# Smaller PSUM tiles, a new order of convolution bursts, and a moved share of the statistics in a ConvNeXt-V2 block

**Chip, cores, metric.** One core of a Trainium2 chip. The time is device microseconds of one execution, median of several; lower is better.

## The reference

```python
# x: (1, 512, 512, 96) bf16
out = depthwise_conv_3x3(x, dw)
h = layernorm(out, axis=-1)
h = gelu(h @ w1)                                   # 96 -> 384, tanh form
gx = sqrt((h*h).sum(axis=(1, 2)) + 1e-6)           # over all pixels, by channel
nx = gx / (gx.mean(-1) + 1e-6)
h = grn_gamma * (h * nx) + grn_beta + h
return x + h @ w2                                  # 384 -> 96
```

The sum of squares over all pixels is needed before the contraction may start. So the kernel has two phases: phase 1 makes `h` block by block (128 blocks of four rows) for the sum, and phase 2 makes most of `h` again and contracts it.

## The kernel before

`# ...` marks cuts. A block has four quarters of 512 pixels. For channel-major quarters (channels on partitions) VectorE's `bn_stats` gives the sum of squares; for the others (pixel-major) TensorE adds `v.T @ v` to a Gram matrix, whose diagonal is the sum.

```python
def cm_quads(q):                      # channel-major quarters of block q
    return 2 if is_res(q) else 3      # is_res: the last two blocks
# PSUM: psS 1 bank (Gram and layernorm sums, one tile SG),
#       psU 2 tiles of 2 banks, psY 1 tile of 3 banks (convolution)
psU = p1.enter_context(tc.tile_pool(name="psU", bufs=2, space=bass.MemoryType.PSUM))

def burst(n, fence=True):             # 24 matmuls of the convolution
    # ...
    if n < 2 and fence:
        pe.drain()

def pair(j):                          # two quarters of one chunk of 128 channels
    U = psU.tile([128, 2, QW], f32, name="U")
    for t in range(2):
        cm_mm(U[:, t, :], j, t)
    act.activation(out=gsh[:, :, j, :], in_=U[:], func=ACTF.Gelu_apprx_tanh)
# rest(n): the same for 1024 columns of the third and fourth quarter, into gm

def stage_moments(k):                 # once in a batch of four blocks
    # ...
    dve.tensor_scalar(out=m[:, :, :N], in0=S[:, :, :N], scalar1=1.0 / C, scalar2=None, op0=ALU.mult)
    dve.memset(S[:], 0.0)             # S is a part of SG

def combine(b):                       # when 32 entries of bn_stats are full
    # ... for j in range(NCH): dve.bn_aggr(...)

# one slot: convolution of block s beside the expansion of an earlier block b
conv(0); pair(0); conv(1); spread_out(); turn_x(s + 2)
pair(1); squares(0); gram_of_last(0)
pair(2); squares(1); gram_of_last(1)
rest(0); squares(2); stage_turn(k); conv(2); evac()   # evac: y_bf <- Y on ScalarE
rest(1); stage_stats(b2); rest(2); squares_rest()
for b in get("combine"):
    combine(b)                        # then the next slot, first its stage_moments
```

The program gives each engine its instructions in this order.

## Time and profile before

| | before |
|---|---|
| time, median of 3 runs | 1563.49 us (1561.01 to 1563.60) |
| phase 1 and phase 2 | about 1024 us and 535 us |
| one ordinary block of phase 1 | 7.40 us |

### The profile page before, as it was taken

Reading aid. Unit: us, or ns where it says so; the run is one execution under the profiler, and the core shown is the slowest. Engines: PE = TensorE matmul, PEld = TensorE weight load, DVE = VectorE, ACT = ScalarE, POOL = GpSimd, SP = SyncE. Lnnn points to the kernel's source line nnn. Section 1 sums busy time; section 2 is a strip of 40 time slices with the busy share of each in tenths; the row PEclk is TensorE's granted clock in tenths of the full one; section 3 lists DMA queues with packets and bytes.
Section 4 is the critical chain, followed back from the end, with each engine's and each line's share of the span. In section 5 each row is a group of like instructions: output and inputs, shape, how many; then the busy total and the mean of one; then the engine's idle time right before and its main releaser. Section 6 shows DMA issues by size and latency. Waiting matters only on the chain. (4 is left out here: it accounts for less than half of the span.)

```text
span 1559.3 us, 54608 instructions
## 1 busy us (share of the span) xinstructions
PE 1438.9 (92%) x23119; PEld 819.7 (53%) x23119; DVE 1211.7 (78%) x2157; ACT 1436.7 (92%) x1306; POOL 1318.4 (85%) x933
## 2 busy tenths in 40 slices
PE   7889989999999999999999997789999999999998
PEld 3334444444444444444444443357777766676666
DVE  6749989999999999999999999955555555455555
ACT  3779989999999999999999999999999999899997
POOL 3459889989998998898899897459999999899997
PEclk8899999999999999999999999999999999999999
DMA  5568787777778778778868767879999999999996
GB/s 152 162 174 256 241 251 249 223 225 246 228 245 250 231 226 258 237 221 250 244 207 252 221 198 222 275 249 395 380 385 384 381 377 378 341 389 379 376 379 236
DMA packets 235467, 427.86 MB, mean 274 GB/s; under 512 B 34103, under 2 KB 148375, under 8 KB 235223
## 3 DMA queue, kind: packets, MB, share of 16 engines
q1 hardware_dynamic: 219972, 356.59, 70.4%
q0 software_dynamic: 13888, 67.64, 11.5%
q8 instruction: 181, 2.97, 0.8%
q14 instruction: 64, 0.52, 0.1%
q10 hardware_dynamic: 1362, 0.15, 0.1%
HBM read 272.78 MB, written 150.72 MB: 272 GB/s over the span
## 5 line engine op out<-in xcount | busy, mean ns | idle before, releaser
L32 PE MATMUL U<-ynT,w1p 128*128 128x512 bf16 x2292 | 664.4, 381 | 48.5 <-ACT gm L32 10.0
L32 ACT ACTIVATE gr<-U 128x1536 bf16<-128x1536 f32 (+1 forms) x384 | 519.1, 1456 | 13.1 <-PE U L32 11.3
L32 DVE BATCH_NORM_STATS2 bst<-gsh 128x6 f32<-128x512 bf16 x756 | 463.0, 674 | 21.7 <-ACT gsh L32 15.7
L32 DVE TENSOR_TENSOR o_sb<-O,xb 128x384 bf16<-128x384 f32 x512 | 277.9, 556 | 250.7 <-PE O L32 153.0
L32 POOL TENSOR_TENSOR yn<-y_bf,rbc 128x1536 bf16<-128x1536 bf16 x128 | 397.4, 3107 | 87.3 <-ACT rbc L32 31.0
L32 ACT ACTIVATE gsh<-U 128x1024 bf16<-128x1024 f32 x378 | 374.5, 1025 | 61.5 <-PE U L32 61.4
L278 POOL TENSOR_TENSOR xb<-xr,B2c 128x1536 f32<-128x1536 bf16 x126 | 394.8, 3135 | 33.9 <-DVE B2c L32 30.9
L32 ACT ACTIVATE gm<-U 128x1024 bf16<-128x1024 f32 x384 | 381.8, 1047 | 0.2
L32 PE MATMUL Y<-xT,Wq 64*32 64x511 bf16 (+1 forms) x8694 | 324.6, 391 | 32.9 <-ACT y_bf L32 25.8
L32 POOL TENSOR_TENSOR ysq<-y_bf 128x1536 bf16<-128x1536 bf16 x114 | 313.2, 2748 | 32.9 <-ACT y_bf L32 32.4
L32 PEld LDWEIGHTS <-w1p 128*128 128x128 bf16 x2292 | 181.6, 97 | 289.5 <-issue 203.3
L32 PEld LDWEIGHTS <-gr 128*128 128x128 bf16 x4584 | 236.8, 98 | 107.5 <-issue 23.4
L32 PE MATMUL O<-W2s,gr 128*128 128x96 bf16 x4584 | 257.2, 206 | 12.4 <-DVE o_sb L32 11.9
L32 DVE BATCH_NORM_STATS2 bst<-gm 128x6 f32<-128x512 bf16 x378 | 242.3, 679 | 29.7 <-ACT gm L32 29.7
L32 PEld LDWEIGHTS <-Wq 64*32 64x32 bf16 x9216 | 114.0, 91 | 212.5 <-issue 174.1
L32 ACT ACTIVATE y_bf<-Y 128x1536 bf16<-128x1536 f32 x121 | 177.5, 1467 | 16.2 <-PE Y L32 16.1
L32 DVE STREAM_TRANSPOSE xT<-xin 128x576 f32<-128x576 f32 (+1 forms) x256 | 180.4, 745 | 2.1 <-DMA xin<-in_x_dram 2.0
L32 PEld LDWEIGHTS <-gm 128*128 128x128 bf16 x1560 | 106.8, 98 | 66.3 <-issue 11.7
L32 PE MATMUL SG<-gm 128*128 128x128 bf16 x1560 | 126.1, 219 | 8.9 <-DVE SG L32 8.2
L32 PE MATMUL U<-w1p,ynT 128*128 128x384 bf16 (+2 forms) x780 | 126.5, 272 | 5.0 <-ACT gm L32 3.8
L250 POOL DMA_DIRECT2D xr<-in_x_dram x123 | 68.4, 556 | 35.9 <-POOL xb L278 35.9
L32 PEld LDWEIGHTS <-ynT 128*128 128x128 bf16 x780 | 67.3, 97 | 35.3 <-issue 15.4
(103 smaller groups left out, 696.6 us busy)
## 6 DMA issues: line engine op xcount, KB each, us to landing
ynT<-yn_dram SPq DMA_DIRECT2D x254, 384.0 KB
xin<-in_x_dram SPq DMA_DIRECT2D x126, 432.0 KB
yn_dram<-yn SPq DMA_DIRECT2D x512, 96.0 KB
xr<-in_x_dram POOLq DMA_DIRECT2D x128, 384.0 KB, 6.5
out_dram<-o_sb SPq DMA_DIRECT2D x127, 384.0 KB
g_dram<-gsh SPq DMA_DIRECT2D x126, 384.0 KB
gl<-g_dram SPq DMA_DIRECT2D x84, 384.0 KB
gl<-g_dram POOLq DMA_DIRECT2D x42, 384.0 KB, 7.2
```

Source lines behind the costliest of these rows:

```text
L32: r = f(*a, **k)
L250: pq.dma_start(out=xr[:], in_=x[0, r0:r0 + GR].rearrange("r w c -> (r w) c").rearrange("(p g) c -> p g c", g=PXP))
L278: pq.tensor_tensor(out=xb[:], in0=grp[q]["xr"][:], in1=bias[:, None, :].to_broadcast([128, PXP, C]), op=ALU.add)
```

## The change

Its intent: give ScalarE work while TensorE runs a convolution burst. Three tiles (2, 1 and 1 banks) take the place of two tiles of 2 banks. A tile and a half are filled before the second burst instead of one, that burst has no drain behind it, and the Gram matmuls move later. Two channel-major quarters instead of three in every third block take work from VectorE and give it to TensorE; this part is called "the third" below. A "meeting" below is a place where VectorE has the aggregation directly ahead of the moments of a batch.

```diff
     def cm_quads(q):
-        return 2 if is_res(q) else 3
+        return 3 if q % 3 and not is_res(q) else 2
...
-        psU = p1.enter_context(tc.tile_pool(name="psU", bufs=2, space=bass.MemoryType.PSUM))
+        psU2 = p1.enter_context(tc.tile_pool(name="psUa", bufs=1, space=bass.MemoryType.PSUM))
+        psU1 = p1.enter_context(tc.tile_pool(name="psUb", bufs=2, space=bass.MemoryType.PSUM))
+        def banks(n):
+            return (psU2 if n == 2 else psU1).tile([128, n, W], f32, name=f"U{n}")
...                                            (pair and rest become unit(first bank, banks))
                 conv(0)
-                pair(0)
-                conv(1)
+                unit(0, 2)
+                unit(2, 1)
+                squares(0)
+                conv(1, False)
                 spread_out()
                 if s + 2 < NBLK:
                     turn_x(s + 2)
-                pair(1)
-                squares(0)
-                ...                            (gram_of_last(0))
-                pair(2)
+                unit(3, 1)
+                unit(4, 2)
                 squares(1)
-                ...                            (gram_of_last(1))
-                rest(0)
+                gram_of_last(0)
+                unit(6, 1)
                 squares(2)
+                unit(7, 1)
                 ...
                 conv(2)
                 if evac:
                     evac()
-                rest(1)
+                gram_of_last(1)
+                unit(8, 2)
+                unit(10, 1)
                 ...                            (statistics)
-                rest(2)
+                unit(11, 1)
                 squares_rest()
```

More of the change, by code (lines that the diff above doesn't have):

```diff
@@ L260, in fresh, with half @@
                     grp[q]["made"] = late.gr.tile([128, NCH, (NQ - 1) * QW], bf16, name="gr")
-                if is_res(q):
-                    U = psU.tile([128, 2, QW], f32, name="U")
-                else:
-                    U = late.psU2.tile([128, NQ - 1, QW], f32, name="U2")
-                for t in range(nk, NQ):
-                    pe.matmul(quad_out(U[:, t - nk, :]), lhsT=w1p[:, j * 128:(j + 1) * 128],
-                               rhs=quad(ynt[:], t), start=True, stop=True)
-                n = (NQ - nk) * QW
-                act.activation(out=grp[q]["made"][:, j, :n], in_=U[:].rearrange("p k w -> p (k w)")[:, :n],
-                                func=ACTF.Gelu_apprx_tanh)
+                def half(U, t0, t1):
+                    for t in range(t0, t1):
+                        pe.matmul(quad_out(U[:, t - t0, :]), lhsT=w1p[:, j * 128:(j + 1) * 128],
+                                  rhs=quad(ynt[:], t), start=True, stop=True)
+                    act.activation(out=grp[q]["made"][:, j, (t0 - nk) * QW:(t1 - nk) * QW],
+                                   in_=U[:, :t1 - t0, :].rearrange("p k w -> p (k w)"), func=ACTF.Gelu_apprx_tanh)
+                if not is_res(q):
+                    half(late.psU2.tile([128, NQ - 1, QW], f32, name="U2"), nk, NQ)
+                elif j % 2:
+                    half(banks(1), nk, nk + 1)
+                    half(banks(1), nk + 1, NQ)
+                else:
+                    half(banks(2), nk, NQ)
             return [lambda j=j: fresh(j) for j in range(NCH)]
@@ L344 @@
         busy(FILL[0])
-        Ud = psU.tile([128, 2, W], f32, name="U")[:, 0, :NI * 9].rearrange("p (i k) -> p i k", i=NI)
+        Ud = banks(2)[:, 0, :NI * 9].rearrange("p (i k) -> p i k", i=NI)
         for i in range(NI):
@@ L409, in conv_taps @@
             if spare:
-                Ua = psU.tile([128, 2, W], f32, name="U")
-                Ub = psU.tile([128, 2, W], f32, name="U")
+                Ua, Ub = banks(2), banks(1)
                 Y = [Ua[:, 0, :], Ua[:, 1, :], Ub[:, 0, :]]
@@ L538, in stage_spread @@
             wide = rns.pop(k)
-            U = psU.tile([128, 2, W], f32, name="U")
+            U = banks(2)
             for bb in range(n):
@@ L617, in cm_mm, with unit @@
                 pe.matmul(quad_out(dst), lhsT=w1p[:, j * 128:(j + 1) * 128], rhs=quad(yt[:], t), start=True, stop=True)
-            def pair(j):
-                U = psU.tile([128, 2, QW], f32, name="U")
-                for t in range(2):
-                    cm_mm(U[:, t, :], j, t)
-                act.activation(out=gsh[:, :, j, :], in_=U[:], func=ACTF.Gelu_apprx_tanh)
-            def rest(n):
-                U = psU.tile([128, 2, QW], f32, name="U")
+            def unit(bank, n):
+                U = banks(n)
+                if bank < 2 * NCH:
+                    j, t0 = divmod(bank, 2)
+                    for t in range(t0, t0 + n):
+                        cm_mm(U[:, t - t0, :], j, t)
+                    act.activation(out=gsh[:, t0:t0 + n, j, :], in_=U[:], func=ACTF.Gelu_apprx_tanh)
+                    return
                 Uf = U[:].rearrange("p k w -> p (k w)")
-                c0 = 2 * QW * n
-                c, end = c0, c0 + 2 * QW
+                c = c0 = (bank - 2 * NCH) * QW
+                end = c0 + n * QW
                 while c < end:
@@ L660, in store @@
                 sp.dma_start(out=g_dram[b], in_=gsh[:, 0].rearrange("p j w -> p (j w)"))
-            return pair, rest, squares, squares_rest, store
+            return unit, squares, squares_rest, store
         def gram_mms(b, part=None):
@@ L780 @@
                 b = mlp[0]
-                pair, rest, squares, squares_rest, put_out = mlp_units(b)
+                unit, squares, squares_rest, put_out = mlp_units(b)
                 conv = lambda n, fence=True: taps[n](fence) if taps else None
@@ L794 @@
                     turn_x(s + 2)
-                pair(1)
-                squares(0)
-                if not taps:
-                    gram_of_last(0)
-                    gram_of_last(1)
-                if taps:
-                    gram_of_last(0)
-                pair(2)
+                unit(3, 1)
+                unit(4, 2)
                 squares(1)
-                if taps:
-                    gram_of_last(1)
-                rest(0)
+                gram_of_last(0)
+                unit(6, 1)
                 squares(2)
+                unit(7, 1)
                 for k in get("turn"):
```

## The prediction

> **What bounds the kernel now.** I read first the windows view, to see where the time lies. The kernel has two phases: up to about 1024 us it convolves, normalises, expands and gathers statistics, after that it expands again and contracts.
>
> ```profile
> core 0: us, PE busy (x) PEld busy (x) DVE busy (x) ACT busy (x) POOL busy (x), PEclk, DMA share, GB/s
> 400.00:600.00 200.00, 185.88 (x3280) 90.42 (x3286) 191.65 (x324) 185.65 (x187) 178.21 (x138) 1.00 0.78 240
> 1100.00:1200.00 100.00, 99.58 (x1406) 72.78 (x1403) 54.22 (x100) 99.71 (x75) 92.42 (x56) 1.00 1.04 384
> ```
>
> In phase 1 four engines are 89 to 96% busy and none is full. In phase 2 TensorE and ScalarE are full; the change leaves that phase as it is (it alters only what the two last blocks use there), so I leave its 535 us alone. Second, the waits between 200 and 1000 us:
>
> ```profile
> ACT gsh L32 <- PE U L32: 51.3, 106, 1.5
> PE Y L32 <- ACT y_bf L32: 20.2, 96, 0.7
> PE SG L32 <- DVE SG L32: 8.2, 8, 1.6
> ```
>
> The first is one bubble of ScalarE in every block. Third, the timeline of one block (start, length, engine, instruction, idle before it) shows where it comes from:
>
> ```profile
> 606.97 1.97 ACT L32 ACTIVATE gm<-U 128x1024 bf16<-128x1024 f32 x2
> ...
> 607.16 0.88 PE L32 MATMUL Y<-xT,Wq 64*32 64x512 bf16 x24 [0.20 <-ACT y_bf L32]
> ...
> 608.16 0.60 PE L32 MATMUL U<-ynT,w1p 128*128 128x512 bf16 x2
> ...
> 608.69 0.87 PE L32 MATMUL Y<-xT,Wq 64*32 64x512 bf16 x24
> 608.85 1.02 ACT L32 ACTIVATE gsh<-U 128x1024 bf16<-128x1024 f32 x1
> ...
> 609.67 0.60 PE L32 MATMUL U<-ynT,w1p 128*128 128x512 bf16 x2
> ...
> 610.31 1.94 ACT L32 ACTIVATE gsh<-U 128x1024 bf16<-128x1024 f32 x2 [0.44 <-PE U L32]
> ...
> 612.14 1.03 ACT L32 ACTIVATE gm<-U 128x1024 bf16<-128x1024 f32 x1
> ...
> 613.04 1.47 ACT L32 ACTIVATE y_bf<-Y 128x1536 bf16<-128x1536 f32 x1
> ...
> 614.37 1.97 ACT L32 ACTIVATE gm<-U 128x1024 bf16<-128x1024 f32 x2
> ```
>
> A block takes 614.37 - 606.97 = 7.40 us. ScalarE runs without a gap except once: after the first gsh tile it waits until 610.31, because TensorE had to start from the end of y_bf (614.51 in the next block, which frees the convolution's only PSUM tile), run a conv burst, the first pair, a second burst, and only then the second pair. So the ring y_bf -> conv -> pair -> conv -> pair -> gsh -> gm -> y_bf sets 7.40.
>
> **What the skill says.** "ScalarE: Activation LUTs", section "What ACT_TABLE_LOAD costs", gives 186 ns + 0.833 ns an element with immediates, and about 93 ns of overlap between neighbours, hence some 93 ns of fixed cost in a dense row. The trace is kinder: dense gm tiles start 0.904 us apart and y_bf takes 1.331, so 0.051 us is fixed; I use that. "TensorE: Matmul & The Clock Gate", section "Wait — 56ns, not 53.3ns?", gives 215.7 ns from one 512-column matmul to the next; a pair here takes 0.432 us, which agrees. The same page's "Architectural detail: the array is 16× 32×32, not 1× 128×128" says that VectorE's queue is strict FIFO[...]; the stall below agrees with it.
>
> **The change part by part**, for a block, with T = 0 at the end of y_bf.
>
> *ScalarE.* Six tiles of 1024 become three of 1024 and six of 512. The dense row was 6 x 0.904 + 1.331 = 6.76; it becomes 3 x 0.904 + 6 x (512 x 0.833 + 51 = 0.477 us) + 1.331 = 6.91. Three instructions cost 0.15 us; the bubble of about 0.5 (0.44, plus the lost overlap) is what can be won, with some 0.13 of other slack.
>
> *TensorE's steps*, from starts in the trace: burst with its drain 0.98, without 0.81, two banks 0.43, one bank 0.215, entering a burst 0.10 more, half the Gram matmuls 0.335, all statistics 0.60. The new order runs: conv0 0.05, first tile of two banks 1.03 (ready for ScalarE at 1.03 + 0.60 + 0.09 = 1.72), one bank 1.46, conv1 without drain 1.78, one bank 2.59 (ready 3.05), two banks 2.81 (ready 3.50), Gram 3.24, banks 3.58 and 3.79, conv2 4.11 to 4.92. ScalarE wants these at 1.72, 2.62, 3.10, 3.58, 4.48, 4.96, and y_bf at 5.44: all are just in time, so the bubble closes, and y_bf ends at 6.90. TensorE itself needs 6.75. **An ordinary block falls from 7.40 to about 6.90.**
>
> *The third with two channel-major quarters.* Three BatchNorm statistics of VectorE go (3 x 0.63 = 1.9 us; VectorE is at 7.0 of 7.4 us a block, so without this it would become the bound). Their sums move into the Gram matrix: 12 more matmuls, 2 x 0.335 = 0.67 us of TensorE, in the block after. TensorE then needs 6.75 + 0.67 = 7.42, and that block takes about 7.44. Mean (2 x 6.90 + 7.44) / 3 = 7.08; over some 110 blocks with convolution 110 x 0.32 = 35 us.
>
> *What gives some of it back.* The last ten to twelve blocks without convolution are ScalarE-bound at 5.55 us and pay the three instructions: about +2 us. The larger thing is in VectorE's order. In these lines of before the aggregation of 32 statistics stood directly ahead of the moments of a batch of four blocks:
>
> ```profile
> 322.97 2.77 DVE L32 BATCH_NORM_AGGREGATE mv<-bst 128x2 f32<-128x192 f32 x3
> ...
> 325.65 0.23 DVE L32 TENSOR_SCALAR mom<-SG 128x128 f32<-128x128 f32 x1
> ...
> 325.98 0.17 DVE L32 MEMSET SG<- 128x128 f32 x1
> ...
> 326.20 0.49 PE L32 MATMUL SG<-gm 128*128 128x128 bf16 x6 [1.63 <-DVE SG L32]
> ...
> 327.17 1.02 ACT L32 ACTIVATE gsh<-U 128x1024 bf16<-128x1024 f32 x1 [1.53 <-PE U L32]
> ```
>
> The Gram matmuls share the SG tile with the moments and wait for its memset, and ScalarE then waits for TensorE. The reader is to see a 9.05 us block, 1.65 over. With three entries a block, 32 entries are 10.67 blocks, so aggregation and moments met only three times (and nearly met three times, +0.9): 8 us in all. With 8 entries in three blocks, 32 entries are exactly 12 blocks, three batches: the instruction order of the changed kernel shows aggregation directly ahead of moments eight times. VectorE is also later there: its transposes now stand behind the first squares, which wait for the first gsh tile (end 2.75); 9 x 0.63 + 1.42 = 7.1 us later, in the next block at about 3.1, the statistics end, then aggregation 2.77, moments and memset 0.5: 6.4, where the Gram wants to start at 3.24. That is 2.9 us of block time, eight times: 24 us against 8, so +16.
>
> Sum: -35 + 2 + 16 = -17 us: **1546 us**.
>
> **The rivals.** (a) *The meeting costs little*, because VectorE is further ahead than I think or TensorE finds the time again. VectorE has a statistic less a block on average, which speaks for it; against it, the path SG -> Gram -> next tile -> ScalarE cost its full 1.65 in before. Then about 1530. (b) *GpSimd becomes the bound.* It has 178 of 200 us, 6.6 a block, and about 0.3 more are gaps within its chains of small dependent instructions: 6.9 to 7.0. At a mean of 7.3 it should hide; at 7.08 there is hardly room, so it limits rival (a). (c) *The just-in-time steps fail*: at 3.10 and 3.58 ScalarE has only 0.05 to 0.08 us in hand; if each is missed by 0.1, an ordinary block is 7.1, and the whole gain is near zero: 1560. (d) *TensorE is the bound in more blocks*, since twelve pieces of matmul with small columns replace nine: +0.1 in a third of the blocks, +4 us.
>
> **Range and chances.** The middle is 1546. Rival (a) alone goes to 1530, together with less Gram cost to 1527; (c) and (d) go to 1560. Over 2% faster means below 1532.2, which needs rival (a) nearly whole: 17%. Over 2% slower needs a new bound of more than 7.7 us a block, for which I see nothing: 4%.
>
> **What would show it.** In the profile after: dense gsh rows without the 0.44 wait, and y_bf about 6.90 apart twice and 7.44 once in every three blocks; VectorE's BatchNorm statistics on gm fewer by 126; Gram matmuls more by 504; the wait of SG for VectorE up from 8 to some 25 us with eight blocks near 9.8 us; phase 2 unchanged at 535 us. The prediction is wrong if y_bf stays above 7.2 in ordinary blocks (rival c), if the eight blocks are under 8.5 us (rival a), or if GpSimd's yn ends the waits of the expansion's loads (rival b).

## More of the kernel before

For the comparison later, three groups of the profile's page: line, engine, operation, output and inputs, shapes, count, then busy time in us and the mean in ns, then idle time ahead of them and what ended it.

```profile
L32 ACT ACTIVATE gsh<-U 128x1024 bf16<-128x1024 f32 x378 | 374.5, 1025 | 61.5 <-PE U L32 61.4
L32 DVE BATCH_NORM_STATS2 bst<-gm 128x6 f32<-128x512 bf16 x378 | 242.3, 679 | 29.7 <-ACT gm L32 29.7
L32 PE MATMUL SG<-gm 128*128 128x128 bf16 x1560 | 126.1, 219 | 8.9 <-DVE SG L32 8.2
```

The 61 us in the first line are ScalarE's idle time that the change is after.

## The result and the profile after

Before 1563.55 us (4 runs), after 1550.91 us (4 runs, 1548.86 to 1556.72): ratio 0.9928, 95% interval 0.9898 to 0.9957. A ratio here is the mean time of one kernel's fast runs over that of the other's of the same rounds, so it is not quite the ratio of the medians. So the change is 0.7% faster. The sum of the prediction, 1546 us, was 5 us too low; the steps follow.

**The bubble closed.** First the waits from 200 to 1000 us (who waited for whom, total us, times, longest), then the timeline of a block after:

```profile
PE SG L32 <- DVE SG L32: 17.8, 8, 2.3
ACT gm L32 <- PE U L32: 16.5, 9, 2.3
ACT gsh L32 <- PE U L32: 1.4, 2, 1.0
```

```profile
604.10 2.98 ACT L32 ACTIVATE gsh<-U 128x1024 bf16<-128x1024 f32 x4
604.16 0.86 PE L32 MATMUL Y<-xT,Wq 64*32 64x512 bf16 x24
604.96 0.86 PE L32 MATMUL U<-ynT,w1p 128*128 128x512 bf16 x3
...
606.88 1.18 ACT L32 ACTIVATE gm<-U 128x512 bf16<-128x512 f32 x2
...
607.87 1.53 ACT L32 ACTIVATE y_bf<-Y 128x1536 bf16<-128x1536 f32 x1
...
609.22 2.08 ACT L32 ACTIVATE gm<-U 128x1024 bf16<-128x1024 f32 x3
...
611.60 2.92 ACT L32 ACTIVATE gsh<-U 128x1024 bf16<-128x1024 f32 x4 [0.30 <-ACT gm L32]
```

ScalarE now works through the second burst (604.16): four gsh tiles follow without a gap, and its wait for TensorE there fell from 51.3 us to 1.4. Only in the block in which TensorE has the extra Gram matmuls is there a gap, 0.30 ahead of 611.60. It is booked on "ACT gm", which had ended just before; the tile it lacked came from TensorE, which began the convolution late. Read off the starts of y_bf, blocks repeat as 6.97, 7.06 and 7.46 us, 7.16 in the mean, against 7.40. By the ends of y_bf, which run 3 shows to be the better measure, they are 7.03, 7.03 and 7.43.

**The eight meetings are there.** The timeline where aggregation stands ahead of the moments:

```profile
619.33 2.76 DVE L32 BATCH_NORM_AGGREGATE mv<-bst 128x2 f32<-128x192 f32 x3
...
622.33 0.17 DVE L32 MEMSET SG<- 128x128 f32 x1
...
622.55 0.49 PE L32 MATMUL SG<-gm 128*128 128x128 bf16 x6 [2.25 <-DVE SG L32]
...
623.36 1.08 ACT L32 ACTIVATE gm<-U 128x512 bf16<-128x512 f32 x2 [1.81 <-PE U L32]
```

TensorE waits 2.25 us for VectorE's memset, and ScalarE 1.81 for TensorE. This block took 9.1 us. In five of the eight the loss was larger, though the wait was no longer (2.0 to 2.3 us in all eight): three blocks took 10.4 to 10.7, two took 9.3 and 9.9 with 1 us more in the block after. Windows over a short and a long one (PEclk, the granted TensorE clock, is the third column from the end), and the matmuls of a burst in the two (count, busy us, mean ns):

```profile
615.30:624.50 9.20, 6.71 (x124) 3.31 (x123) 9.10 (x16) 7.38 (x12) 7.51 (x8) 1.00 0.87 286
703.50:714.20 10.70, 8.22 (x125) 4.00 (x124) 10.60 (x18) 7.30 (x12) 7.79 (x12) 0.84 0.86 277
```

```profile
L32 PE MATMUL Y<-xT,Wq 64*32 64x511 bf16 x16 | 0.7, 384 | 0.0
L32 PE MATMUL Y<-xT,Wq 64*32 64x511 bf16 x16 | 1.1, 628 | 0.0
```

In the long one TensorE comes out of its wait at a lower clock: mean 0.84 over the block, and matmuls of 628 ns instead of 384 just after. Adding over the three blocks from each meeting what exceeds 6.97 + 7.06 + 7.46 gives 2.2 us three times and 3.5 to 3.75 five times, together 24.6; the five are those with a mean clock below 1. What sets these five apart stands in the last section.

The page's three groups again:

```profile
L32 ACT ACTIVATE gsh<-U 128x1024 bf16<-128x1024 f32 x504 | 373.1, 855 | 14.5 <-ACT gm L32 11.1
L32 DVE BATCH_NORM_STATS2 bst<-gm 128x6 f32<-128x512 bf16 x252 | 156.2, 675 | 0.5 <-ACT gm L32 0.5
L32 PE MATMUL SG<-gm 128*128 128x128 bf16 x2064 | 160.3, 222 | 18.3 <-DVE SG L32 17.8
```

The counts moved by -126 and +504, as worked out. From the end of the last gm tile to the end of the program lie 541.9 us before and 542.1 after: phase 2 did not change.

### The profile page after: what moved, and what is told of

It reads as the page before. It is cut to its first block, busy times and chain, and to the rows that moved or that the text cites. A ratio compares the mean times of both kernels' runs of the same rounds, so it can differ in the third digit from the quotient of the medians.

```text
span 1554.9 us, 56008 instructions
## 1 busy us (share of the span) xinstructions
PE 1448.7 (93%) x23749; PEld 849.9 (55%) x23749; DVE 1128.7 (73%) x2027; ACT 1454.4 (94%) x1692; POOL 1315.8 (85%) x933
## 5 line engine op out<-in xcount | busy, mean ns | idle before, releaser
L32 PE MATMUL U<-ynT,w1p 128*128 128x512 bf16 x2166 | 607.4, 380 | 35.8 <-ACT gm L32 7.5
L32 ACT ACTIVATE gr<-U 128x1536 bf16<-128x1536 f32 (+1 forms) x386 | 519.7, 1449 | 12.6 <-PE U L32 11.0
L32 ACT ACTIVATE gm<-U 128x512 bf16<-128x512 f32 (+1 forms) x640 | 412.2, 765 | 16.7 <-PE U L32 16.5
L32 PEld LDWEIGHTS <-w1p 128*128 128x128 bf16 x2166 | 171.5, 97 | 239.5 <-issue 138.2
L32 PEld LDWEIGHTS <-Wq 64*32 64x32 bf16 x9216 | 109.0, 91 | 198.9 <-issue 153.6
L32 ACT ACTIVATE y_bf<-Y 128x1536 bf16<-128x1536 f32 x121 | 183.8, 1519 | 25.4 <-PE Y L32 23.2
L32 PEld LDWEIGHTS <-gm 128*128 128x128 bf16 x2064 | 128.9, 99 | 103.1 <-issue 72.1
L32 PE MATMUL SG<-gm 128*128 128x128 bf16 x2064 | 160.3, 222 | 18.3 <-DVE SG L32 17.8
L32 PE MATMUL U<-w1p,ynT 128*128 128x384 bf16 (+2 forms) x1032 | 164.1, 276 | 1.7 <-ACT gsh L32 0.6
L32 DVE BATCH_NORM_STATS2 bst<-gm 128x6 f32<-128x512 bf16 x252 | 156.2, 675 | 0.5 <-ACT gm L32 0.5
L32 PEld LDWEIGHTS <-ynT 128*128 128x128 bf16 x1032 | 81.8, 99 | 31.0 <-issue 7.0
```

The lines of the kernel that those rows point to most:

```text
L32: r = f(*a, **k)
```

## The experiments

Ten runs of nine kernels, all correct, each five rounds against the kernel before on the same chip. Time is the median; the 95% intervals of the ratios reach 0.001 to 0.003 to either side.

| run | us | ratio to before |
|---|---|---|
| the change again | 1550.85 | 0.9942 |
| aggregation one block later | 1525.97 | 0.9779 |
| without the third | 1538.22 | 0.9855 |
| the third alone | 1584.06 | 1.0148 |
| drain put back | 1559.49 | 0.9991 |
| old tiles, new order, third, drain | 1572.23 | 1.0080 |
| every fourth block instead of third | 1528.81 | 0.9799 |
| every eighth, aggregations spread | 1523.69 | 0.9753 |
| the same again | 1523.50 | 0.9767 |
| none, aggregations spread | 1523.73 | 0.9770 |

Before was 1559.95 (first four), 1561.15 (next four), 1559.56 (last two).

**1. The change again**, no edit.

> The changed kernel once more, as the control for the others. The profile of its first run had, between 85 and 92 us, a stretch with TensorE at a low clock that cost some 4 us against the kernel before; its four times ran from 1548.9 to 1556.7. If that stretch belongs to one run, the profile now lacks it and the median is 1549 to 1552; if it belongs to the kernel, it is there again. In steady state: y_bf again 6.97, 7.06 and 7.46 us apart, and eight blocks of 9.1 to 10.7 us.

Measured 1550.85 us. The slow stretch was absent (the block from 77.5 us took 9.3 instead of 14.0), so it belongs to a run. It is some of the scatter of about 10 us between runs of this kernel. In it TensorE stands idle for 3.92 us, which the profile puts down to no other engine and no transfer, and then has a clock of 0.69 to 0.73 in the mean; the cause of the idle time stays open. The eight long blocks were there again, three of them with the lower clock, and cost 21.7 us together.

**2. Aggregation one block later.**

```diff
-                put(m, "combine", b)
+                put(m + (b < NBLK - 1), "combine", b)
```

> Changed kernel, with each aggregation of 32 statistics emitted one block later, so that it no longer stands ahead of the moments. My theory: the eight blocks of 9.1 to 10.7 us go (they and their successors cost 24.7 us in the profile against the pattern of 21.5 us for three blocks), nothing else changes: 1551 - 24 = 1527 us, no wait of SG for DVE above 0.5 us. Rival: the eight stalls only gave GpSimd time to catch up (it has about 6.9 of 7.16 us a block); then GpSimd takes their place and the time is 1540 or more, with waits for yn on the way.

Measured 1525.97 us, 25 below the change, 1 below the forecast. The waits from 200 to 1000 us have no entry of SG for VectorE left, and the blocks go on as 6.97, 7.08, 7.45 through the places of the former stalls. The timeline at one of these places shows the moments' memset first, Gram matmuls without a wait, and the aggregation only after them:

```profile
603.92 0.17 DVE L32 MEMSET SG<- 128x128 f32 x1
...
604.36 0.50 PE L32 MATMUL SG<-gm 128*128 128x128 bf16 x6
...
608.83 2.77 DVE L32 BATCH_NORM_AGGREGATE mv<-bst 128x2 f32<-128x192 f32 x3
```

So the meetings cost 25 us by the medians, and GpSimd did not take their place. The same instructions, one line moved, are worth two to three times what the change had brought (12.6 and 9.1 us).

**3. Without the third.**

```diff
-        return 3 if q % 3 and not is_res(q) else 2
+        return 2 if is_res(q) else 3
```

> Changed kernel with three channel-major quarters in all blocks as before (tiles and order of the change kept). Theory: TensorE's extra 0.67 us in every third block goes, so the blocks of 7.46 us go; VectorE now has 1.20 + 1.35 + 2.35 + 1.78 = 6.7 us a block from the steps in the trace, with aggregation and moments 7.1, just over ScalarE's 7.04. So some 7.1 to 7.15 a block, three meetings of aggregation and moments instead of eight (-15 us): about 1533 us. Rival (the intent of the change): VectorE becomes the bound, its lag makes the Gram matmuls wait for SG after every batch, 7.4 us a block and 1560 us or more.

Measured 1538.22 us, 5 above the forecast and far from the rival's 1560. Ordinary blocks are 7.04 apart, where I had 7.10 to 7.15, and ScalarE has no gap at all in them (timeline of ScalarE):

```profile
565.14 2.99 ACT L32 ACTIVATE gsh<-U 128x1024 bf16<-128x1024 f32 x4
567.92 1.19 ACT L32 ACTIVATE gm<-U 128x512 bf16<-128x512 f32 x2
568.88 1.58 ACT L32 ACTIVATE y_bf<-Y 128x1536 bf16<-128x1536 f32 x1
570.21 2.15 ACT L32 ACTIVATE gm<-U 128x1024 bf16<-128x1024 f32 x3
572.18 2.99 ACT L32 ACTIVATE gsh<-U 128x1024 bf16<-128x1024 f32 x4
```

Take the ends, not the starts: 568.13, 569.11, 570.46, 572.36, 575.17. The steps are 0.98 for two small tiles, 1.35 for y_bf, 1.90 for one large and two small, 2.81 for two and two: 7.04 together, just the block. That is ScalarE's floor with these tiles. Three full meetings (blocks of 9.7 to 9.8 us) and smaller stalls in seven more blocks (8.4 to 8.8) make the rest. That VectorE, without a short block, recovers slowly from an aggregation would explain these. No run tests that alone, but run 9, which spreads the aggregations of this kernel, has no ordinary block over 8.2 us and is 14 us faster. The third thus cost 12.6 us beside the change's other parts.

**4. The third alone** (on the kernel before, the one line of `cm_quads`).

> Kernel before with only the third of blocks with two channel-major quarters. Theory: TensorE's 12 more Gram matmuls stand in the ring between the pairs of the old order and cost about 0.43 us in every third block (16 us), and the aggregation meets the moments eight times at 1.65 us instead of three and three (+5): 1563 + 21 = 1584 us. Rival: VectorE's 95% share was what held the old block at 7.40; then taking 8% of its work away makes it faster than 1555.

Measured 1584.06 us, as forecast. Every third block takes 7.84 instead of 7.40, a step of 0.44, and the eight meetings take 9.05 (six), 9.25 and 10.51. The waits from 200 to 1000 us:

```profile
ACT gsh L32 <- PE U L32: 58.8, 111, 2.2
PE SG L32 <- DVE SG L32: 13.2, 9, 1.6
```

ScalarE's wait for TensorE did not fall though VectorE has less to do, and the blocks between stayed at 7.40. VectorE, busy for 95% of the time, was not what held the ordinary old block.

**5. The drain put back** (on the change).

```diff
-                conv(1, False)
+                conv(1)
```

> Changed kernel with the drain after the second conv burst put back. Theory: it adds 0.18 us to TensorE's row; in the blocks that TensorE bounds (7.46) all of it shows, in the others ScalarE has about 0.1 us in hand at the fourth tile, so some 0.05 to 0.11 shows: mean +0.11 x 110 blocks = +12: 1551 + 12 = 1563 us, blocks of 7.05, 7.15 and 7.64. Rival: the steps have more in hand than I read; then only the third block shows it, +7: 1557 us or less.

Measured 1559.49 us, 3.5 below the forecast: blocks of 7.06, 7.16 and 7.57 by starts. By the ends of y_bf they are 7.06, 7.12 and 7.60, against 7.03, 7.03 and 7.43 without the drain. So the third block pays nearly all of the 0.18 us, and the others pay 0.03 and 0.09: they have 0.15 and 0.09 in hand. By the difference to run 1 the removed drain is worth some 9 us of the change (8 by the ratios).

**6. Old tiles in the new order** (on the kernel before, with the third).

```diff
                 conv(0)
                 pair(0)
+                pair(1)
+                squares(0)
                 conv(1)
                 ...
-                pair(1); squares(0); gram_of_last(0)
                 pair(2)
                 squares(1)
-                gram_of_last(1)
+                gram_of_last(0)
                 rest(0)
                 ...
                 conv(2)
                 evac()
+                gram_of_last(1)
                 rest(1)
```

> Kernel before with the third of blocks and the change's order (two expansions ahead of the second burst), but with its two tiles of two banks; the drain stays, for without it the check finds a race. To be compared with the run that has the drain back: the tile split alone lies between them. Theory: the second pair must wait for a tile until the old gm tile is read (1.88 instead of 1.46 us after y_bf), so the second burst and the third pair come late, ScalarE is idle some 0.3 us there: 7.36 us in two blocks and 8.05 in the third, 7.6 in the mean, 1598 us: the split is worth some 36 us at the same order. Rival: the order alone closes the bubble; then within 8 us of the run with the drain back.

Measured 1572.23 us, 12.7 above the run with the drain back, where I expected 36. The timeline shows the two waits that I named:

```profile
611.40 0.59 PE L32 MATMUL U<-ynT,w1p 128*128 128x512 bf16 x2 [0.18 <-ACT gm L32]
611.92 0.87 PE L32 MATMUL Y<-xT,Wq 64*32 64x512 bf16 x24
...
613.55 1.02 ACT L32 ACTIVATE gsh<-U 128x1024 bf16<-128x1024 f32 x1 [0.30 <-PE U L32]
```

The second pair waits 0.18 us for its tile, and ScalarE 0.30 for the third pair. Blocks are 7.31 to 7.39 where I had 7.36, but the third block takes 7.56, not 8.05: I added the Gram matmuls to a row in which TensorE had waits, and they went into those. So the split is worth 13 us at the same order and drain; with it goes that three banks instead of four are filled ahead of the second burst. By run 4 against this one, the new order alone is worth 12 us. These two figures are rough, since a lower clock followed seven meetings in this profile, three in run 5's and one in run 4's. By the ends of y_bf outside the meetings, the mean block falls by 0.12 us with the order, 0.16 with the split and 0.10 with the missing drain.

**7. Every fourth block.**

```diff
-        return 3 if q % 3 and not is_res(q) else 2
+        return 2 if is_res(q) or q % 4 == 3 else 3
```

> Changed kernel with two channel-major quarters in every fourth block (the last of each batch of four) instead of every third. Aggregation then falls due every 11.6 blocks and never stands directly ahead of the moments; mostly it stands one short block ahead. Theory: the eight stalls of over 2 us go without moving any instruction by hand; VectorE is still about 0.5 us late in seven blocks (+4); the pattern is 3 x 7.04 + 7.44 = 28.6 for four blocks, 7.14 a block, -2: 1551 - 25 - 2 + 4 = 1528 us. Rival: the stall is the price of aggregation wherever it stands: then 1545 us or more.

Measured 1528.81 us. The stalls of over 2 us are gone, with the aggregation emitted by the same code: what matters is only where the count of entries lets it fall.

**8. A better version: every eighth block, aggregations spread.**

```diff
+        return 2 if is_res(q) or q % 8 == 3 else 3
...
-                        dve.bn_aggr(out=mv[:, j, k, :], in_=...)
+                        owed.append((mv[:, j, k, :], ...))
...                                              (at the end of each slot)
+            for _ in range(len(owed) if s == last_slot else min(len(owed), 1 if s % 4 != 1 else 0)):
+                o, i_ = owed.pop(0)
+                dve.bn_aggr(out=o, in_=i_)
```

> Attempt at a better version: every eighth block with two channel-major quarters, and the three aggregations of one set handed out one a block, never in the block ahead of the moments. Theory: ScalarE's floor of 7.04 in seven blocks of eight and 7.45 in one, 7.09 a block against 7.16 (-8), no stalls (-24): 1519 us. VectorE has about 6.9 us a block, so it just fits. Rival: VectorE lags, waits of SG of 0.5 us or more after the batches: 1526 us or more.

Measured 1523.69 us: faster than the kernel before by 2.5%. Blocks are 7.03 and 7.43 as forecast. Four were still 7.3 to 7.75; with the blocks after them they cost 2.3 us of the 4.7 by which the forecast was too low, and the rest stays open.

**9 and 10. The same with no such block, and the same again.** The edit of 9 is `return 2 if is_res(q) else 3` in the version of 8.

> The better version without any block of two channel-major quarters apart from the last two: does that part of the change earn its place once the aggregation no longer meets the moments? Theory: ScalarE's floor is 7.04 us a block, VectorE needs 6.7 + 0.25 + 0.15 = 7.1, so VectorE just becomes the bound and the moments run late: 7.1 us or a little more a block with waits of SG after the batches, 1524 to 1530 us, no better than with every eighth block (1523.7). Rival: buffers hide VectorE's lag; then 110 x 0.05 = 6 us faster, 1518 us.

> The better version again, on the same chip as its sister without the eighth: 1521 to 1525 us, blocks of 7.03 and 7.43, no wait of SG above 0.7 us.

Measured 1523.73 and 1523.50 us: no difference. The windows of the two, 9 first:

```profile
400.00:600.00 200.00, 190.67 (x3461) 93.05 (x3468) 198.08 (x340) 198.41 (x282) 187.89 (x142) 1.00 0.82 251
400.00:600.00 200.00, 192.84 (x3520) 96.46 (x3519) 193.72 (x331) 198.39 (x282) 189.04 (x148) 1.00 0.83 253
```

ScalarE (fourth busy column) is full at 198.4 of 200 in both. Without the eighth VectorE is full too (198.08), and TensorE waits longer for SG (8.7 us between 200 and 1000 us, 1.3 at the longest, against 2.4 and 0.8 in run 10, for which I had set 0.7), which can account for what the missing Gram matmuls save. Once ScalarE is the floor, moving statistics between the other engines gained nothing here.

## Why the prediction was right, by its steps

- **The ring and its bubble: right.** The wait of 0.44 us went with the new order (result). By the runs, new tiles, order and missing drain alone are worth 22 us (run 3 against before). With the third in place they are worth 33 (run 4 against run 1): some 12 for the order, 13 for the split and 9 for the drain (runs 4, 6, 5 and 1, each against the next).
- **An ordinary block of 6.90: wrong by 0.1, and this is the term that was mis-sized.** I took ScalarE's dense row from starts 0.904, 0.477 and 1.331 apart. An instruction's recorded start runs ahead into the one before it, a little further each time (13 ns here); ends are 0.917, 0.490 and 1.344 apart (run 3), so the fixed cost is 0.063 us a tile, not 0.051. The row of 10 is 7.04, not 6.91. The old row was 6.85, not 6.76, so the bubble was 0.55 us and most of the "0.13 of other slack" was not there; the three instructions cost 0.19, not 0.15. The pattern became 7.16 instead of 7.08: over 110 blocks 9 us of the -35.
- **The third at 7.44: right** (7.46). That it would earn its place I took as given, since VectorE "would become the bound" without it. It does not: the change is 12.6 us slower with it, and ordinary blocks without it stay at ScalarE's 7.04 (run 3), though ten blocks have stalls. Where the aggregations are kept off the moments, it hardly matters: 1525.97 us with it (run 2), 1523.73 without (run 9).
- **The tail, +2: right.** From the end of the last y_bf of the convolution to the end of the last gm lie 81.1 us before and 83.2 after.
- **The meetings, 24 us against 8: right in the sum** (24.6 and 21.7 in two profiles, 25 by run 2), but by luck, out of two errors. The wait of TensorE was 2.25 us, not the 3.15 that I had from 3.24 to 6.4: VectorE's statistics ended 0.6 earlier than I had set (2.5 us after the end of y_bf, not 3.1); that the block ahead was one of 7.43 us, and not of 6.90, would account for most of it. Against it stood a lower TensorE clock after five of the waits, which I had not thought of: 3.5 to 3.75 us lost instead of 2.2.
- **Rival (a)**, meetings that cost little, fell with run 2. **Rival (b)**, GpSimd, fell as well: in run 10 it works 189 of 200 us and blocks still keep ScalarE's 7.03. **Rival (c)** was half true: the steps have 0.09 to 0.15 us in hand (run 5), enough. **(d)** was not seen: by ends, ordinary blocks stand at ScalarE's 7.03.

With the corrected terms: -26 for the blocks, +2 for the tail, +17 for the meetings, -7 in all; the two measured differences are -12.6 and -9.1, and the start of the program scatters by 4 us either way between profiles.

## What to carry to other kernels

When a change shifts how often a periodic instruction falls due, work out where in the queue it will land: an aggregation of 2.8 us cost some 8 us where it fell due every 10.67 blocks, and 25 us where it fell due every 12, exactly three batches. Take the dense rate of an engine from the ends of its instructions, not from their starts. Before work is moved off an engine that is 95% busy, ask whether that engine ends any wait on the ring: here it ended none in an ordinary block, and the move cost 24 us in the old order (run 4) and 13 in the new (run 3).

## What the Trainium skill lacked or had wrong

- "ScalarE: Activation LUTs" (section "What ACT_TABLE_LOAD costs"): 186 ns less 93 of overlap would leave a fixed cost of some 93 ns in a dense row. The section does not say which memory is read; the tiles here are read from PSUM. The skill's own figure for that is another, about 51 ns, in "Perfetto Trace Analysis" (section "Optimizing Scalar/DVE Operations"), which the prediction did not use. The runs show 63 ns between ends (0.490 us for 512 elements, 0.917 for 1024, 1.344 for 1536).
- No page that I used says that the recorded start of an ACTIVATE drifts ahead in a dense row (51 ns by starts, 63 by ends), so that starts alone understate its cost.
- "TensorE: Matmul & The Clock Gate" (Part 1, "What's actually happening") has the array go cold after an idle window of about 3.4 us. Here waits of 2.0 to 2.3 us were followed by a lower clock in five of eight cases in one profile and three of eight in the next (0.84 in the mean of one such block, matmuls of 628 ns against 384), and not in the others. The trace shows what sorts them. Each stretch of lower clock lasts 3.413 us, and in the first profile they begin 26, 52, 130 and 182 times 3.413 us after the first. If the time is cut into such intervals, TensorE is idle for 1.79 to 2.26 us of the one just ahead of each of the eight drops. In the other eight cases an edge between intervals divides the wait so that no interval has more than 1.73 us idle. So an interval need not be idle throughout. The exact limit is not shown: in other runs intervals with 1.7 to 1.9 us idle went both ways.
